# Putting a slot's four products of scores and maxima next to one another in an attention and GEGLU kernel

## The chip, the cores and the metric

The kernel runs on one core of a Trainium2 chip. Its time is device time in microseconds (us), from runs on the chip; the profile is one more execution, taken with the hardware profiler.

## The reference

For 2048 tokens of width 576 it computes a residual step with attention gated by a feed-forward network:

```
xn = layernorm(x)
s  = softmax(q k^T / sqrt(18)) v, over 32 heads of width 18, then @ wo      (q, k, v = xn @ wqkv)
g  = silu((gelu(xn @ w_gate) * (xn @ w_up)) @ w_down)                        (inner width F = 4608)
out = x + s * g
```

Everything is in float32.

## The kernel before

Float32 products are made of pieces: an operand is split into a high and a low part in TensorE's faster format, and two or three products of parts are added up. So a product with q and k takes its parts stacked in 54 rows of one tile, and one of gate or up takes three products over 64 rows for each 64 rows of the width.

**Order of the work.** A first part normalises x, makes q, k and v and stores them in DRAM. What follows is one long sequence of 144 *sections*, each of which computes one tile of 128 columns of F for one block of 512 tokens (4 blocks, 36 tiles each). The function `section` (L455) takes `gate_up` (L377) for 27 *steps*: one step is a product for `pg` on rows 0 to 63 and one for `pu` on rows 64 to 127, which run side by side. Attention is woven into these sections. TensorE's order is the order of the program (`manual_schedule` for that engine); the other engines and the DMA queues are ordered by a planner, which keeps the program's order only where `keep_in_program_order` asks for it.

**Attention.** A *unit* is four heads for one block of 512 queries; there are 32 units (NU), each with 32 *slots* (NS), eight to a section, so a unit takes four sections (NA). The softmax subtracts the true maximum of each row, so a unit's maxima are computed ahead of its scores: `LEAD` is 40 slots, five sections. The nine opening sections compute the first maxima alone (`lead_pair`), and the last five sections with attention have no maxima left. A slot has:

- two scores (`score_mm`, L716): a product `pe` of keys by queries with the negated maximum as two more rows, on rows 0 to 55 or 64 to 119, that ScalarE empties with an exp into `pT` (L725);
- two maxima (`max_mm`, L685): a product `pm` of queries by keys on rows 0 to 53 or 64 to 117, that VectorE empties with a reduce to a column of `mx` (L694).

`slot_pairs` (L732) makes two *pairs* of them: the score of one half of the rows with the maximum of the other half. Each pair is one step of TensorE. `spread` (L56) puts a section's list of specials between its 27 steps of gate and up.

**Behind the steps of a section** come, in this order on TensorE: `values` (L750), which multiplies the section's exps with v into an accumulator `acc`; in the third section of a unit `max_end` (L704), which transposes the maxima of a coming unit through a product with an identity into a `pm` (L707) that VectorE copies to `mr` (L709); at some places a part of the output projection (`project_o`); and in every second section the products with w_down (`down`, L414) of the last two tiles of F, whose `py` VectorE adds to `Y` (L431). At the last pair of F tiles of a block these are divided over two sections (`finish`, L489). `acc` goes to `accs` after four key tiles by ScalarE (L763) and afterwards by VectorE's add (L765). The activation of gate and up takes three operations each of ScalarE and VectorE (`activate`, L397; its last on VectorE is L408).

**PSUM.** There are eight buffers of 512 columns in three groups (`BANKS`): two for `pg` and `pu` (tag f), three for `pe` and `py` (tag s), three for `pm`, `acc` and `po` (tag m). A group's buffers are used in turn; a product into one waits until what its former contents were read by is done. The wait stands at the load of the product's weights.

**GpSimd** splits the weights of the next section in three tiles (`split_gu`, L93 and L95; five buffers each) and each section's activation. DMAs are issued from SyncE behind the section's steps (`load_k`, `load_v`, `load_q`) and ahead of them (`load_gu`).

Of the kernel before, what the change touches and what calls it, by code (L numbers as in the profile page):

```python
# [30 lines left out]
NU = NQ * NB  # L31
NS = 2 * NT
SLOTS = 8
# [18 lines left out]
def f(ap):  # L52
    return ap.bitcast(F32)


def spread(pairs, specials):  # L56

    n, m = len(pairs), len(specials)
    out = []
    for i in range(n):  # L60
        out += specials[i * m // n:(i + 1) * m // n]
        out.append(pairs[i])
    return out

# [2 lines left out]
def kernel(ctx: ExitStack, tc: tile.TileContext, x, wqkv, wo, w_gate, w_up, w_down, out):  # L67
    nc = tc.nc
    x = x.rearrange("b s d -> (b s) d")
    out = out.rearrange("b s d -> (b s) d")  # L70
# [35 lines left out]
    def raw_tile(shape, pool=wts):  # L106
        return pool.tile(shape, F32, name="raw", tag="raw", bufs=2)

    def load_gu(t, keep=lambda i: i):

        raw = raw_tile([P, NC, P])
        for a, w in enumerate((w_gate, w_up)):
            keep(nc.sync.dma_start(raw[HR * a:HR * a + HR], w[:, t * P:(t + 1) * P].rearrange("(k p) n -> p k n", p=HR)))
        return raw, [], []

    def split_gu(w, k):
        hi, lo = (wts.tile([P, XG, P], F32R, name=m, bufs=5) for m in ("wh", "wl"))
        split(hi, lo, w[0][:, XG * k:XG * k + XG, :])
        w[1].append(hi)
        w[2].append(lo)  # L120

    def load_xd(b):

        xd = [[], []]
        for c in range(0, NC, XG):
            for i in range(2):
                t = wts.tile([P, XG, TB], F32R, name=f"xd{i}_{c}")
                nc.sync.dma_start(f(t)[0:HR], xhs[b][i, c * HR:(c + XG) * HR, :].rearrange("(k p) t -> p k t", p=HR))
                nc.gpsimd.tensor_copy(t[HR:P], t[0:HR])
                xd[i].append(t)  # L130
        return xd
# [8 lines left out]
    with tc.tile_pool(name="pro", bufs=1) as pro, tc.tile_pool(name="pps", bufs=1, space=PSUM) as pps:  # L140
# [109 lines left out]
        def split_qk(t, raw):  # L250
            hi, lo = (pro.tile([P, KT, P], F32R, name=f"q{m}{t}") for m in "hl")
            first = split(hi, lo, raw)
            put_qk(t, hi, lo)
            return first
# [77 lines left out]
        for b in range(NB):  # L332
            for n, t in enumerate(ORDER):
                if n == (2 if b == 0 else 0) and b + 1 < NB:
                    xr = load_x(b + 1)
                if b == 0 and ahead_qk:
                    first = split_qk(*ahead_qk.pop(0))
# [39 lines left out]
    def gate_up(tag):  # L377

        w, xd = FF["w"], FF["xd"]
        pg, pu = (ps.tile([P, TB], F32, name=n, tag=tag, bufs=BANKS[tag]) for n in ("pg", "pu"))  # L380
        terms = [(wp, *divmod(c, XG), xp) for c in range(NC) for wp, xp in ((0, 0), (1, 0), (0, 1))]

        def pair(i):
            wp, k, c, xp = terms[i]
            for a, o in enumerate((pg, pu)):
                rr = slice(HR * a, HR * a + HR)
                nc.tensor.matmul(o, w[1 + wp][k][rr, c, :], xd[xp][k][rr, c, :], start=(i == 0),  # L387
                                 stop=(i == len(terms) - 1))

        return [lambda i=i: pair(i) for i in range(len(terms))], pg, pu  # L390
# [6 lines left out]
    def activate(pg, pu, early):  # L397

        t1 = ffn.tile([P, TB], F32, name="t1", bufs=2)
        nc.scalar.activation(t1, pg, AF.Square)  # L400
        nc.vector.scalar_tensor_tensor(t1, t1, 1.0 / GC, pg, op0=ALU.add, op1=ALU.mult)
        if early:
            t2 = ffn.tile([P, TB], F32, name="t2", bufs=1)
            nc.scalar.activation(t2, pu, AF.Copy)
            nc.vector.tensor_tensor(t2, t2, pg, op=ALU.mult)
        nc.scalar.activation(t1, t1, AF.Tanh, scale=GC * GS)
        if early:
            nc.vector.scalar_tensor_tensor(t1, t1, 1.0, t2, op0=ALU.add, op1=ALU.mult)  # L408
        else:
            nc.vector.scalar_tensor_tensor(t1, t1, 1.0, pg, op0=ALU.add, op1=ALU.mult)  # L410
            nc.vector.tensor_tensor(t1, t1, pu, op=ALU.mult)
        return t1
# [39 lines left out]
            nc.sync.dma_start(ys[rows, cc], th)  # L452
        FF["gates"] = []

    def section(specials=(), tag="f", raw_d=None, early=None):  # L455

        n = FF["n"]
        FF["n"] += 1
        b, r = divmod(n // G, NR)
        g = n % G  # L460
        pairs, pg, pu = gate_up(tag)
        if g == 0:
            FF["hs"] = []
        keep = tc.keep_in_program_order if n == NU * NA + len(FIRST) + 1 else lambda i: i
        nxt = load_gu((n + 1) % (NR * G), keep) if n + 1 < NF else None
        if nxt:
            for k in range(NG - 1):
                split_gu(nxt, k)
        if g == G - 1:
            raw = FF["rawd"] = raw_d() if raw_d else raw_tile([P, G, D])  # L470
            nc.sync.dma_start(raw, w_down[r * G * P:(r + 1) * G * P, :].rearrange("(g p) n -> p g n", p=P))
            if early:
                FF["wd"] = early(raw)
        for p in spread(pairs, specials):
            p()
        if nxt:
            split_gu(nxt, NG - 1)
        FF["w"] = nxt
        if n + 1 < NF and (n + 1) % (NR * G) == 0:
            FF["xd"] = load_xd(b + 1)  # L480
        FF["act"] = activate(pg, pu, n < ATT.stop)
# [118 lines left out]
    def tasks(n, part):  # L600
        for t in todo.pop((n, part), []):
            t()
# [3 lines left out]
    for b in range(NB):  # L606
# [9 lines left out]
        first = (b + 1) * AB + 3 if last else max((b + 1) * AB + 6, (b + 1) * NR * G - len(FIRST) + 5)  # L616
# [4 lines left out]
        for i in range(GROUPS):  # L621
            n = first + i * (1 if last else G)
# [17 lines left out]
    with tc.tile_pool(name="att", bufs=1, reuse_waits="tile") as att:  # L640
# [44 lines left out]
        def max_mm(u, i, a):  # L685

            if u not in MX:
                MX[u] = att.tile([P, QD, 4, 4], F32, name="mx", bufs=2)
            i, r = divmod(i, 2)
            c, t = divmod(i, 4)  # L690
            rr = slice(64 * a, 64 * a + MROW)
            pm = ps.tile([P, TB], F32, name="pm", tag="m", bufs=3)
            nc.tensor.matmul(pm, QS[u, r][rr, t * P:(t + 1) * P], KS[(u * NA + c) % KB][r][rr, :], start=True, stop=True)  # L693
            nc.vector.tensor_reduce(MX[u][:, 2 * r + a, t, c:c + 1], pm, axis=AX.X, op=ALU.max)  # L694
# [21 lines left out]
        def score_mm(u, i, a, tag="s"):  # L716

            kt, r = divmod(i, 2)
            if r == 0 and a == 0:
                PT[u, kt] = att.tile([P, QD, TB], F32, name="pT", bufs=4)  # L720
            rr = slice(64 * a, 64 * a + MROW + 2)
            pe = ps.tile([P, TB], F32, name="pe", tag=tag, bufs=BANKS[tag])
            c, t = divmod(kt, VC)
            nc.tensor.matmul(pe, KS[(u * NA + c) % KB][r][rr, t * P:(t + 1) * P], QS[u, r][rr, :], start=True, stop=True)  # L724
            nc.scalar.activation(PT[u, kt][:, 2 * r + a, :], pe, AF.Exp, scale=SCALE)  # L725
# [6 lines left out]
        def slot_pairs(s):  # L732

            u, i = divmod(s, NS)
            um, im = divmod(s + LEAD, NS)

            def pair(h):
                for a in range(2):
                    if a == h:
                        score_mm(u, i, a)  # L740
                    elif um < NU:
                        max_mm(um, im, a)

            def alone():
                for a in range(2):
                    score_mm(u, i, a, "sm"[a])

            return [lambda h=h: pair(h) for h in range(2)] if um < NU else [alone]

        def values(u, kt):  # L750
            j, g = divmod(u, NQ)
# [67 lines left out]
        for n in range(NU * NA):  # L819
            u, i = divmod(n, NA)  # L820
            s0 = n * SLOTS
            section([p for s in range(s0, s0 + SLOTS) for p in slot_pairs(s)])
            if n > 0:
                load_k(n - 1 + KB)
            if i == 1 and u + 2 < NU:
                load_q(u + 2)
            gates()
            if n == NA:
                nc.gpsimd.memset(OT, 0.0)
                nc.gpsimd.memset(f(OW[1])[HR:P, KT, :], 0.0)  # L830
            tasks(n, 0)
            um, im = divmod(s0 + LEAD + SLOTS, NS)
            if im == 0 and um <= NU:
                max_neg(um - 1)
            for kt in range(i * SLOTS // 2, (i + 1) * SLOTS // 2):
                values(u, kt)
            load_v(n + 2)
            if im == 0 and um <= NU:
                max_end(um - 1)
            tasks(n, 1)  # L840
            downs()
            tasks(n, 2)
            finish()


    with tc.tile_pool(name="epi", bufs=1, reuse_waits="tile") as epi:
# [4 lines left out]
        n = NU * NA  # L851
# [5 lines left out]
        def early(raw):  # L857
            wd = [epi.tile([P, G, D], F32R, name=m, bufs=2) for m in ("dh", "dl")]
            cut(*wd, raw)
            return wd  # L860
# [36 lines left out]
        for i in range(HIND + 1, GROUPS):  # L897
            th, j, cc = late[i]
# [31 lines left out]
```

## Time and profile before

| | us |
|---|---|
| median of three runs | 2614.52 |
| lowest and highest | 2613.62, 2616.57 |
| the profiled execution | 2613.15 |
| its span, first to last instruction | 2611.4 |

The page gives busy time by engine, the chain of work that ended last and the costliest groups of instructions. In a group, what stands before the bar is line, engine, operation, the tiles written and read, their shapes and the number of instructions; behind it are the busy time in us, the mean length of one in ns, and the idle time of the engine just before them with what ended it. A row of the timeline is start and length in us, engine, line, operation, tiles, count, and in brackets idle time before it and what ended that. PE is TensorE's products, PEld its loads of weights, DVE VectorE, ACT ScalarE, POOL GpSimd. A row of the table by windows is the window, its length, the busy time of PE, PEld, DVE, ACT and POOL with the number of their instructions, the granted clock, the DMA engines' share and GB/s. A step is written as a pair of rows (`pg` with `pu`, `pe` with `pm`) with one start time.

### The profile page before, as it was taken

How to read it: one execution, taken by the hardware profiler on the slowest of the kernel's cores; microseconds unless marked ns; L12 is line 12 of the kernel's file. 1: busy time of each engine (PE TensorE's matmuls, PEld its weight loads, DVE VectorE, ACT ScalarE, POOL GpSimd, SP SyncE). 2: the span in 40 equal slices, each digit the busy share in tenths (PEclk: the TensorE clock that was granted, in tenths of full speed). 3: DMA queues.
4: the chain of work that ended last, by engine and by line, in shares of the span. 5: the costliest groups of instructions: out<-in, count | busy, mean ns of one | idle time of the engine just before them, and what ended most of it. 6: DMA issues, size and time to landing. Idle time of an engine off the chain costs nothing.

```text
span 2611.4 us, 56340 instructions
## 1 busy us (share of the span) xinstructions
PE 2606.0 (100%) x20982; PEld 1930.9 (74%) x20982; DVE 2030.6 (78%) x3501; ACT 1506.9 (58%) x2715; POOL 1388.3 (53%) x1506
## 2 busy tenths in 40 slices
PE   9999999999999999999999999999999999999999
PEld 8888777777777777777777777777777777777778
DVE  5327888888887888888888888888888788888445
ACT  3223466666666666555666665556666765565642
POOL 2227554545466455555447655555455755555553
PEclk9999999999999999999999999999999999999999
DMA  8875434433355344544446444445345543545342
GB/s 269 261 240 155 112 102 106 103 98 103 101 126 138 101 107 107 126 112 127 104 111 149 122 106 108 120 106 138 98 108 122 140 110 100 135 110 132 81 115 58
DMA packets 392191, 324.27 MB, mean 124 GB/s; under 512 B 106540, under 2 KB 307244, under 8 KB 391920
## 3 DMA queue, kind: packets, MB, share of 16 engines
q1 hardware_dynamic: 391920, 320.68, 46.4%
q8 instruction: 168, 2.75, 0.5%
q14 instruction: 103, 0.84, 0.1%
HBM read 267.17 MB, written 52.85 MB: 123 GB/s over the span
## 4 chain that ended last, share of the span: by engine, by line
PE 99%; DMA 0%; DVE 0%; POOL 0%; SPq 0%; issue 0%; ACT 0%; POOLq 0%
PE pg L387 34%; PE py L425 18%; PE acc L759 17%; PE pm L693 9%; PE pe L724 9%; PE po L161 7%; PE po L581 2%; PE pu L387 1%; PE pt L222 0%; PE pm L707 0%; DMA raw<-in_B_w_up_dram 0%; DMA pT<-in_B_w_down_dram 0%; DMA xx<-in_A_x_dram 0%; DVE bs L190 0%; SPq L661 0%; POOL wl L95 0%
## 5 line engine op out<-in xcount | busy, mean ns | idle before, releaser
L725 ACT ACTIVATE pT<-pe 128x512 f32<-128x512 f32 x2048 | 1156.1, 599 | 704.7 <-PE pm L693 579.3
L694 DVE TENSOR_REDUCE mx<-pm 128x1 f32<-128x512 f32 x2048 | 1283.6, 683 | 84.1 <-PE pm L693 76.0
L387 PE MATMUL pg<-xd,wh 64*128 64x512 f32 x2592 | 947.6, 397 | 0.0
L387 PE MATMUL pu<-xd,wh 64*128 64x512 f32 x2592 | 947.1, 397 | 0.0
L693 PE MATMUL pm<-KS,q 54*128 54x512 f32 x2048 | 795.5, 393 | 0.0
L724 PE MATMUL pe<-q,KS 56*128 56x512 f32 x2048 | 788.1, 392 | 0.0
L387 PEld LDWEIGHTS pg<-xd,wh 64*128 64x128 f32 x2592 | 483.2, 187 | 144.5 <-issue 28.4
L93 POOL TENSOR_SCALAR wh<-raw 128x384 fp32r<-128x384 f32 x432 | 228.1, 529 | 609.7 <-PE pu L387 366.1
L387 PE MATMUL pg<-xd,wl 64*128 64x512 f32 x1296 | 508.1, 392 | 0.1
L387 PE MATMUL pu<-xd,wl 64*128 64x512 f32 x1296 | 507.7, 392 | 0.0
L387 PEld LDWEIGHTS pu<-xd,wh 64*128 64x128 f32 x2592 | 483.9, 187 | 1.7
L759 PE MATMUL acc<-pT,VS 128*32 128x512 f32 x4096 | 466.0, 595 | 0.0
L95 POOL TENSOR_TENSOR wl<-raw,wh 128x384 fp32r<-128x384 f32 x432 | 441.4, 1023 | 34.2
L693 PEld LDWEIGHTS pm<-KS,q 54*128 54x128 f32 x2048 | 377.6, 185 | 49.7 <-DVE mx L694 4.0
L724 PEld LDWEIGHTS pe<-q,KS 56*128 56x128 f32 x2048 | 372.0, 185 | 38.8
L431 DVE TENSOR_TENSOR Y<-py,Y 128x288 f32<-128x288 f32 x544 | 247.9, 457 | 161.4 <-PE py L425 161.1
L425 PE MATMUL py<-dh,hh 128*128 128x288 f32 x1152 | 346.2, 301 | 0.0
L425 PE MATMUL py<-dh,hl 128*128 128x288 f32 x1152 | 339.7, 295 | 0.0
L425 PE MATMUL py<-dl,hh 128*128 128x288 f32 x1152 | 339.5, 295 | 0.0
L759 PEld LDWEIGHTS acc<-pT,VS 128*32 128x32 f32 x4096 | 120.0, 109 | 275.7 <-issue 272.8
L387 PEld LDWEIGHTS pg<-xd,wl 64*128 64x128 f32 x1296 | 242.2, 187 | 53.6 <-POOL wl L95 0.4
L425 PEld LDWEIGHTS py<-dh,hh 128*128 128x128 f32 x1152 | 216.4, 188 | 39.4 <-issue 37.7
(127 smaller groups left out, 2966.1 us busy)
## 6 DMA issues: line engine op xcount, KB each, us to landing
KS<-qk SPq DMA_DIRECT2D x1536, 36.0 KB
raw<-in_B_w_gate_dram SPq DMA_DIRECT2D x144, 288.0 KB
raw<-in_B_w_up_dram SPq DMA_DIRECT2D x144, 288.0 KB
raw<-in_B_w_down_dram SPq DMA_DIRECT2D x68, 576.0 KB
VS<-vs SPq DMA_DIRECT2D x128, 152.0 KB
qk<-t SPq DMA_DIRECT2D x72, 256.0 KB
q<-qk SPq DMA_DIRECT2D x384, 36.0 KB
xd<-xhs SPq DMA_DIRECT2D x24, 384.0 KB
```

Source lines behind the costliest of these rows:

```text
L93: first = nc.gpsimd.tensor_scalar(hi, raw, 1.0, 1.0, op0=ALU.mult, op1=ALU.mult)
L95: keep(nc.gpsimd.tensor_tensor(lo, raw, f(hi), op=ALU.subtract))
L161: nc.tensor.matmul(o, st, m, start=(i == 0), stop=(i == len(terms) - 1))
L387: nc.tensor.matmul(o, w[1 + wp][k][rr, c, :], xd[xp][k][rr, c, :], start=(i == 0), stop=(i == len(terms) - 1))
L425: nc.tensor.matmul(py, a[:, tt], w[:, g, cc], start=(n == 0), stop=(n == 3 * G - 1))
L431: nc.vector.tensor_tensor(yy, py, yy, op=ALU.add)
L581: nc.tensor.matmul(po[:, 0:288], o[x][:, k, :], ow[w][:, k, :], start=(m == 0), stop=(m == len(terms) - 1))
L693: nc.tensor.matmul(pm, QS[u, r][rr, t * P:(t + 1) * P], KS[(u * NA + c) % KB][r][rr, :], start=True, stop=True)
L694: nc.vector.tensor_reduce(MX[u][:, 2 * r + a, t, c:c + 1], pm, axis=AX.X, op=ALU.max)
L724: nc.tensor.matmul(pe, KS[(u * NA + c) % KB][r][rr, t * P:(t + 1) * P], QS[u, r][rr, :], start=True, stop=True)
L725: nc.scalar.activation(PT[u, kt][:, 2 * r + a, :], pe, AF.Exp, scale=SCALE)
L759: nc.tensor.matmul(ACC[u][32 * a:32 * a + 32, :], VS[(u * NA + c) % VB][:, v:v + 32], pt[:, a, :], start=first, stop=last, skip_group_chec ...
```

## The change

`slot_pairs` returns one function for a slot instead of two for its pairs. `spread` takes a fixed place for the first special, and puts special i of m ahead of step `i * n // m + first`; the sections of attention call it with `first` = 1, the others as before. In the sections with maxima a slot's two pairs (score and maximum, maximum and score) thus stand next to one another, ahead of steps 1, 4, 7, 11, 14, 17, 21 and 24 of gate and up. In the five sections without maxima, where a slot is one pair of two scores, it stands at the same eight places. No product is added or removed.

```diff
-def spread(pairs, specials):
+def spread(pairs, specials, first=None):
     n, m = len(pairs), len(specials)
+    at = [-(-(i + 1) * n // m) - 1 if first is None else i * n // m + first for i in range(m)]
     out = []
     for i in range(n):
-        out += specials[i * m // n:(i + 1) * m // n]
+        out += [p for p, j in zip(specials, at) if i == j]
         out.append(pairs[i])
     return out
...
-    def section(specials=(), tag="f", raw_d=None, early=None):
+    def section(specials=(), tag="f", raw_d=None, early=None, slots=False):
...
-        for p in spread(pairs, specials):
+        for p in spread(pairs, specials, 1 if slots else None):
             p()
...
-            return [lambda h=h: pair(h) for h in range(2)] if um < NU else [alone]
+            def both():
+                for h in range(2):
+                    pair(h)
+
+            return both if um < NU else alone
...
-            section([p for s in range(s0, s0 + SLOTS) for p in slot_pairs(s)])
+            section([slot_pairs(s) for s in range(s0, s0 + SLOTS)], slots=True)
```

## The prediction

> **What bounds the kernel now.** I read the page's sums first, then the two costliest groups on the engines that empty PSUM, then the busy time of single sections, then the timeline where two sections meet.
>
> ```profile
> span 2611.4 us, 56340 instructions
> ...
> PE 2606.0 (100%) x20982; PEld 1930.9 (74%) x20982; DVE 2030.6 (78%) x3501; ACT 1506.9 (58%) x2715; POOL 1388.3 (53%) x1506
> ...
> PE 99%; DMA 0%; DVE 0%; POOL 0%; SPq 0%; issue 0%; ACT 0%; POOLq 0%
> ...
> L725 ACT ACTIVATE pT<-pe 128x512 f32<-128x512 f32 x2048 | 1156.1, 599 | 704.7 <-PE pm L693 579.3
> L694 DVE TENSOR_REDUCE mx<-pm 128x1 f32<-128x512 f32 x2048 | 1283.6, 683 | 84.1 <-PE pm L693 76.0
> ```
> ```profile
> 1302.11:1316.08 13.97, 13.97 (x120) 9.12 (x119) 13.32 (x23) 10.68 (x19) 8.35 (x8) 1.00 0.53 109
> 1316.08:1336.45 20.37, 20.37 (x168) 15.43 (x167) 16.76 (x30) 10.68 (x19) 9.77 (x11) 1.00 0.28 77
> ```
>
> TensorE is busy all the time and is 99% of the chain that ended last. A section without products of w_down (the first of the two) is 13.97 us, one with them 20.37 us, both wholly TensorE at clock 1.00. The change adds and removes no product, so it cannot shorten a TensorE that never waits; it can only leave the time alone or make TensorE wait. VectorE is the neighbour to watch: 13.32 us of work in the 13.97. So the question is whether each product still finds its PSUM buffer free.
>
> ```profile
> 1316.19 0.19 PEld L693 LDWEIGHTS pm<-KS,q 54*128 54x128 f32 x1
> 1316.42 0.19 PEld L387 LDWEIGHTS pg<-xd,wl 64*128 64x128 f32 x1
> 1316.42 0.19 PEld L387 LDWEIGHTS pu<-xd,wl 64*128 64x128 f32 x1
> 1316.65 0.19 PEld L387 LDWEIGHTS pg<-xd,wh 64*128 64x128 f32 x1
> 1316.66 0.19 PEld L387 LDWEIGHTS pu<-xd,wh 64*128 64x128 f32 x1
> 1316.89 0.18 PEld L693 LDWEIGHTS pm<-KS,q 54*128 54x128 f32 x1
> ```
> ```profile
> 1316.42 0.39 PE L693 MATMUL pm<-KS,q 54*128 54x512 f32 x1
> ```
>
> A step (two products on the two halves of the rows) follows the next after 0.2325 us (0.23 or 0.24 in the rows), whether it is of gate and up or of scores and maxima. The weights of a step are loaded one step ahead: those of the first maximum at 1316.19, its product at 1316.42. It is this load that waits for the buffer.
>
> **The change part by part.** *Order.* Before, the 16 pairs of a section stand ahead of gate/up steps 1, 3, 5, 6, 8, 10, 11, 13, 15, 16, 18, 20, 21, 23, 25, 26; after, slots of two pairs stand ahead of steps 1, 4, 7, 11, 14, 17, 21, 24. Counting both kinds, the maxima fall on steps 1, 2, 6, 7, 11, 12, 17, 18, 22, 23, 27, 28, 33, 34, 38, 39 of 43, where they fell on 1, 4, 7, 9 and so on up to 41. Steps of scores directly behind steps of scores (8 in each of 123 sections with maxima, 984) do not occur before. The nearest rows are the mixed neighbours above, 0.23 and 0.24 for 0.2325, so from 5 us less to 7 us more over all; I take nothing, since the rate did not depend on the neighbour.
>
> *Inside the slots.* Maxima have three buffers. A reduce starts 0.46 us after its product, or behind the reduce ahead of it.
>
> ```profile
> 1302.45 0.39 PE L693 MATMUL pm<-KS,q 54*128 54x512 f32 x1
> ```
> ```profile
> 1302.91 10.15 DVE L694 TENSOR_REDUCE mx<-pm 128x1 f32<-128x512 f32 x16 [0.24 <-PE pm L693]
> ```
> ```profile
> 212.87 4.28 DVE L694 TENSOR_REDUCE mx<-pm 128x1 f32<-128x512 f32 x7 [1.37 <-PE pm L693]
> ```
>
> The last row is a jammed stretch: (4.28 - 0.68) / 6 = 0.60 us from reduce to reduce. From the first maximum of a section at 0, products come at 0, 0.23, 1.16, 1.395, 2.325, 2.56. Reduces start at 0.46, 1.06, 1.66 (behind the second; its product alone would allow 1.62). A reduce frees its buffer after 0.68 + 0.06 (the 0.06 is shown below). The fourth maximum needs the first reduce, free at 1.20, which is 0.195 ahead of its product; the sixth needs the third, free at 2.40, 0.16 ahead. A longer gap of four steps then lets VectorE catch up and the pattern starts again. Five loads in a section (maxima 4, 6, 10, 12, 16) thus come 0.04 to 0.07 us later than the usual 0.2325 ahead. What does a late load cost?
>
> ```profile
> 890.14 0.68 DVE L765 TENSOR_TENSOR accs<-acc,accs 128x512 f32<-128x512 f32 x1
> ```
> ```profile
> 890.88 0.18 PEld L693 LDWEIGHTS pm<-KS,q 54*128 54x128 f32 x1 [0.16 <-DVE accs L765]
> ```
> ```profile
> 890.76 0.39 PE L387 MATMUL pu<-xd,wh 64*128 64x512 f32 x1
> 890.99 0.40 PE L693 MATMUL pm<-KS,q 54*128 54x512 f32 x1
> 891.00 0.40 PE L724 MATMUL pe<-q,KS 56*128 56x512 f32 x1
> 891.23 0.39 PE L387 MATMUL pg<-xd,wh 64*128 64x512 f32 x1
> ```
> ```profile
> 1176.30 0.18 PEld L693 LDWEIGHTS pm<-KS,q 54*128 54x128 f32 x1 [0.45 <-DVE accs L765]
> ```
> ```profile
> 1175.89 0.39 PE L387 MATMUL pu<-xd,wh 64*128 64x512 f32 x1
> 1176.30 0.50 PE L693 MATMUL pm<-KS,q 54*128 54x512 f32 x1
> 1176.64 0.39 PE L387 MATMUL pg<-xd,wh 64*128 64x512 f32 x1
> ```
> ```profile
> 1102.88:1125.10 22.22, 22.22 (x183) 17.28 (x182) 17.21 (x31) 10.68 (x19) 11.71 (x14) 1.00 0.33 94
> 1175.08:1197.60 22.52, 22.50 (x183) 17.20 (x182) 17.56 (x32) 10.68 (x19) 11.73 (x15) 1.00 0.34 100
> ```
>
> At 890 the add ended at 890.82, the load went at 890.88 (so 0.06 to release), 0.12 later than its turn at 890.76, and the steps still follow at 0.23: 0.12 is free. At 1176 the load was 0.41 late, the next step came at 1176.64 for 1176.355, and the section took 22.52 for 22.22: 0.41 - 0.12 = 0.29. So the five loads in the slots cost nothing (0.07 under 0.12), with 0.05 us to spare. ScalarE has more: an exp takes 0.60 and three buffers serve it too.
>
> The Trainium skill, TensorEngine Tiling (Array Packing), section PSUM Bottleneck, warns that packing by rows speeds TensorE but not the emptying of PSUM, so that the emptying may become the bound. That speaks against slots of four; by it the time would be that of the first rival below, by the rows the slots cost nothing.
>
> *Where two sections meet.* This is where I find the cost. In the fourth section of a unit the products of maxima come straight behind the values (no products of w_down between). The three buffers then hold the maximum of before (free), the accumulator, and the transposed maxima of the coming unit. The first maximum takes the free one; the second needs the accumulator's.
>
> ```profile
> 1316.12 0.69 DVE L765 TENSOR_TENSOR accs<-acc,accs 128x512 f32<-128x512 f32 x1
> 1316.73 0.27 DVE L709 COPY mr<-pm 32x128 f32<-32x128 f32 x1
> 1316.92 0.23 DVE L790 RECIPROCAL sums<-sums 128x16 f32<-128x16 f32 x1
> 1317.09 0.62 DVE L694 TENSOR_REDUCE mx<-pm 128x1 f32<-128x512 f32 x1
> ```
>
> The add that frees it ends at 1316.81, so the load can go at 1316.87. Today its turn is 1316.89: it fits by 0.02. After the change the second maximum is the step right behind the first, and its load's turn is 1316.42: 0.45 late, 0.12 of it free, 0.33 us lost. Everything on TensorE stands behind that load, the second score of the slot first. VectorE, 0.2 late there (its first reduce at 1317.09 for 1316.88), catches up in the pause.
>
> How often: 32 units have such a section; the last two have no maxima left to compute, and in three (one for each of the first three token blocks, at the last pair of F tiles) w_down's products stand between. That leaves 27. In two of them, the one at 1176 among them, the add is late already: VectorE's chain ahead of it ends late.
>
> ```profile
> 1175.57 0.68 DVE L765 TENSOR_TENSOR accs<-acc,accs 128x512 f32<-128x512 f32 x1
> ```
>
> The last maximum is two steps (0.47) earlier after the change, but the reduces queue; I let the chain gain 0.2 of it. Then the add starts at 1175.37, the load goes at 1176.11 for 1175.42, 0.69 - 0.12 = 0.57 lost, of which 0.29 is lost today: 0.28 each (0.48 with no gain, 0.01 with all of it). Sum: 25 x 0.33 + 2 x 0.28 = 8.8 us.
>
> *The rest.* The first third of the gate and up weights is used up one step later, and GpSimd's split that waits for that is 8.35 us of work in 13.97: covered, and 0.23 us late were it not. DMAs are issued behind the section as before. In the five sections with two products to a slot, slots come two steps earlier at the same rate, and two groups of three buffers take them: nothing. The opening sections keep their places.
>
> **The rivals.** *Evacuation becomes the bound.* If the 0.12 did not hold in slots, the five loads would cost 0.04 + 0.03 + 0.04 + 0.03 + 0.04 = 0.18 us (a stall relieves the next one), x 123 = 22 us, and the meeting 27 x 0.12 = 3 more: 2648. If reduces ran at (10.15 - 0.68) / 15 = 0.63 instead of 0.60, the sixth and twelfth loads would be 0.13 late, 0.01 to 0.02 past the cover: about 4 us, 2627. For it: only 0.05 to spare. Against: the 890 rows.
>
> *Not slower: the copy goes first.*
>
> ```profile
> 1315.90 0.25 PE L707 MATMUL pm<-identr,m 128*32 128x128 f32 x1
> ```
>
> If VectorE's order put the copy of the transposed maxima ahead of the add, it could start 0.06 after that product, at 1316.21, and with its 0.27 and 0.06 to release the buffer would be free by 1316.54, 0.12 behind the load's turn, covered; the accumulator, free at 1317.23, is then due at 1317.35. Cost nothing: 2614.5. It decides from the moment the copy starts ahead of the add. For it: their inputs are ready within 0.2 us of each other. Against: today the add goes first, and the change touches neither.
>
> *Faster: score steps behind score steps are shorter.* The break-even is 8.8 / 984 = 9 ns a step, where the rows show none under 0.23; at 0.22 it would be 984 x 0.0125 = 12 us less, 2611. The Trainium skill, TensorE: Matmul & The Clock Gate, section Back-to-back issue gap, gives 512 / 2.4 + 2.5 = 216 ns for such a product, by which it would be an estimated 2607; every step here is 0.2325, so the trace disagrees.
>
> **How the numbers follow.** The profiled execution took 2613.15 us (span 2611.4), 1.37 under the median of 2614.52. 2613.15 + 8.8 = 2621.95, and at the median 2623.3. Chances: forecast 0.73 (2619 to 2627), evacuation 0.11 (2627 to 2648), copy first 0.09, shorter steps 0.07. The forecast and the evacuation case up to 2636 hold 0.8: range 2618 to 2636. A measurement tells apart about 0.2%, 5.2 us: slower 0.84, same 0.09, faster 0.07.
>
> **What would show it.** Right: loads of maxima waiting for the add of L765 in 27 places, some 0.45 us each; sections like that of 20.37 us growing to 20.70, those of 13.97 unchanged; hundreds of short waits of such loads for L694 that cost no time. Wrong: sections of 13.97 us growing (the slots cost), L709 ahead of L765 (the copy first), or neighbouring score steps off 0.2325.

## The result and the profile after

The changed kernel takes 2622.43 us (median of 7 runs, 2621.50 to 2628.54) where the kernel before takes 2614.00 (median of 7): 1.0034 times as long, 95% interval 1.0022 to 1.0045. The forecast was 2623.3, or 1.0034 at its own median.

The page of the changed kernel (its lines stand one to five further down: L694 is the product of the maxima, L695 their reduce, L770 the add of the accumulator):

```profile
span 2626.8 us, 56338 instructions
...
PE 2615.0 (100%) x20982; PEld 1946.9 (74%) x20982; DVE 2012.3 (77%) x3501; ACT 1463.8 (56%) x2715; POOL 1387.9 (53%) x1506
...
L726 ACT ACTIVATE pT<-pe 128x512 f32<-128x512 f32 x2048 | 1111.4, 597 | 741.5 <-PE pm L694 647.6
L695 DVE TENSOR_REDUCE mx<-pm 128x1 f32<-128x512 f32 x2048 | 1260.2, 682 | 99.6 <-PE pm L694 80.6
```

This execution, 2628.54 us, is the longest of the seven by 5 us, from single long stretches that the experiments below look at again. The same number of products, and the same length of one exp and one reduce: only order and waiting differ. Two sections, the third and the fourth of the unit that was shown of before:

```profile
1311.39:1325.35 13.96, 13.96 (x120) 9.02 (x120) 12.96 (x23) 10.30 (x19) 8.60 (x9) 1.00 0.51 112
1325.35:1346.01 20.66, 20.61 (x168) 15.28 (x167) 16.70 (x30) 10.35 (x19) 9.52 (x11) 1.00 0.27 76
```

13.96 for 13.97 us, and 20.66 for 20.37. The table of waits (engine and line that waited, on whom, us in total, times, longest) names where:

```profile
PEld pm L694 <- DVE accs L770: 14.2, 27, 0.9
...
PEld pm L694 <- DVE mx L695: 3.9, 15, 0.4
```

27 loads of maxima wait for the add of the accumulator, where there were four; waits of such loads for the reduces (15 times, 16 before) are all in the opening sections. The place itself, on VectorE, the loads of weights and TensorE:

```profile
1325.39 0.69 DVE L770 TENSOR_TENSOR accs<-acc,accs 128x512 f32<-128x512 f32 x1 [0.38 <-PE acc L764]
1325.99 0.27 DVE L710 COPY mr<-pm 32x128 f32<-32x128 f32 x1
1326.19 0.23 DVE L795 RECIPROCAL sums<-sums 128x16 f32<-128x16 f32 x1
1326.35 0.62 DVE L695 TENSOR_REDUCE mx<-pm 128x1 f32<-128x512 f32 x1
```
```profile
1325.46 0.19 PEld L694 LDWEIGHTS pm<-KS,q 54*128 54x128 f32 x1
1326.13 0.18 PEld L694 LDWEIGHTS pm<-KS,q 54*128 54x128 f32 x1 [0.48 <-DVE accs L770]
```
```profile
1325.69 0.40 PE L694 MATMUL pm<-KS,q 54*128 54x512 f32 x1
1325.69 0.40 PE L725 MATMUL pe<-q,KS 56*128 56x512 f32 x1
1326.13 0.50 PE L694 MATMUL pm<-KS,q 54*128 54x512 f32 x1
1326.13 0.50 PE L725 MATMUL pe<-q,KS 56*128 56x512 f32 x1
1326.47 0.39 PE L388 MATMUL pg<-xd,wl 64*128 64x512 f32 x1
```

The second maximum's load has its turn when the first one's product starts, 1325.69. The add ends at 1326.08, the load goes at 1326.13, 0.44 late, and the step behind it starts at 1326.47 where 1325.69 + 2 x 0.2325 = 1326.155 was its time: 0.32 us lost. (This section as a whole grew by 0.29; the median of the 27 is 0.32.)

The add itself had to wait: VectorE stood idle for 0.38 us until the accumulator's last product was done. It starts 0.04 us behind the section's start, as it did before (1316.12 and 1316.08); so it is in 22 of the 27 places of either trace. There the load is late by TensorE's own order, and by these rows a faster VectorE ahead of the add would not help.

### The profile page after: what moved, and what is told of

Same layout as the page of the kernel before. It is cut to its first block, busy times and chain, and to the rows that moved or that the text cites. A ratio compares the mean times of both kernels' runs of the same rounds, so it can differ in the third digit from the quotient of the medians.

```text
span 2626.8 us, 56338 instructions
## 1 busy us (share of the span) xinstructions
PE 2615.0 (100%) x20982; PEld 1946.9 (74%) x20982; DVE 2012.3 (77%) x3501; ACT 1463.8 (56%) x2715; POOL 1387.9 (53%) x1506
## 4 chain that ended last, share of the span: by engine, by line
PE 94%; DMA 2%; POOL 1%; DVE 1%; SPq 1%; issue 0%; ACT 0%; POOLq 0%; DVEq 0%
PE pg L388 24%; PE py L426 18%; PE acc L764 16%; PE pu L388 9%; PE pm L694 9%; PE pe L725 8%; PE po L162 7%; PE po L582 2%; DMA raw<-in_B_w_up_dram 1%; DVE accs L770 1%; POOL dl L96 0%; SPq L662 0%; DMA raw<-in_B_w_gate_dram 0%; POOL wl L96 0%; PE pt L223 0%
## 5 line engine op out<-in xcount | busy, mean ns | idle before, releaser
L726 ACT ACTIVATE pT<-pe 128x512 f32<-128x512 f32 x2048 | 1111.4, 597 | 741.5 <-PE pm L694 647.6
L695 DVE TENSOR_REDUCE mx<-pm 128x1 f32<-128x512 f32 x2048 | 1260.2, 682 | 99.6 <-PE pm L694 80.6
L388 PE MATMUL pg<-xd,wh 64*128 64x512 f32 x2592 | 890.1, 398 | 0.9 <-POOL wh L94 0.9
L388 PE MATMUL pu<-xd,wh 64*128 64x512 f32 x2592 | 889.7, 398 | 0.0
L694 PE MATMUL pm<-KS,q 54*128 54x512 f32 x2048 | 643.7, 395 | 2.4 <-DVE accs L770 1.3
L725 PE MATMUL pe<-q,KS 56*128 56x512 f32 x2048 | 641.2, 393 | 0.0
L694 PEld LDWEIGHTS pm<-KS,q 54*128 54x128 f32 x2048 | 376.1, 185 | 93.3 <-DVE accs L770 14.2
L388 PEld LDWEIGHTS pu<-xd,wl 64*128 64x128 f32 x1296 | 241.4, 186 | 10.1
```

## The experiments

Theory A is the prediction's: the loss is the second maximum's load waiting for the accumulator's buffer in 27 fourth sections. Rival B: slots as such make TensorE wait for reduces, a little in each of 123 sections. Rival C: VectorE is late in the fourth section (add, copy and reciprocals stand ahead of its first reduce), whatever buffer is used.

**The first slot's pairs two steps apart, in fourth sections only.**

```diff
-            section([slot_pairs(s) for s in range(s0, s0 + SLOTS)], slots=True)
+            if i == NA - 1 and u + 2 < NU:
+                section(slot_pairs(s0, True) + [slot_pairs(s) for s in range(s0 + 1, s0 + SLOTS)],
+                        slots=[1, 3, 4, 7, 11, 14, 17, 21, 24])
```

> The changed kernel, but in the fourth section of a unit the first slot's two pairs stand ahead of steps 1 and 3, with two steps of gate and up between them; all other slots stay whole. Theory A (the second maximum's weight load waits for the accumulator's buffer): its load has its turn two steps (0.465 us) later than in the changed kernel and finds the buffer free, so the 27 sections fall from 20.69 back to 20.37 us and the time is 2614, give or take 1. Rival B (the slots as such make TensorE wait for reduces, a little in each of the 123 sections): nearly all slots are as before, so the time stays at 2622.

Measured: 2616.83 us, 1.0010 (1.0001 to 1.0020) of the kernel before in the same batch (2614.14). The section of the unit shown:

```profile
1318.33:1338.72 20.39, 20.39 (x168) 15.44 (x167) 16.57 (x30) 10.31 (x19) 9.34 (x11) 1.00 0.25 69
```

One slot of 32 taken apart gives back 5.7 of the 8.4 us, against B. But it stays 2.7 us above the kernel before, outside what was expected (2614, give or take 1). The 27 sections are 0.06 us longer than before in the median, and the attention sections have 56 waits of a maximum's load for a reduce, where the changed kernel has none; see the next run.

**The accumulator in the scores' group of buffers.** Slots stay whole everywhere.

```diff
-                ACC[u] = ps.tile([P, TB], F32, name="acc", tag="m", bufs=3)
+                ACC[u] = ps.tile([P, TB], F32, name="acc", tag="s", bufs=3)
```

> The changed kernel with the accumulator in the PSUM group of the scores (tag s) instead of that of the maxima; order of all engines as in the changed kernel. Theory A: the second maximum no longer needs the accumulator's buffer, so 2614, give or take 1, with all slots whole. Rival B (slots as such): 2622. Rival C (VectorE is late in the fourth section: add, copy and reciprocals stand ahead of its first reduce): its order is the same, so the wait moves to a later maximum of that section and the time stays at about 2622.

Measured: 2615.94, 1.0005 (0.9996 to 1.0015); the same kernel once more, as the base of a later run:

> The run with the accumulator in the scores' group once more, on the same chip as the run with early reciprocals, as its base: 2614.5 to 2616.5, fourth sections at 20.40 us.

It took 2616.14, 1.0007 (0.9998 to 1.0017) of 2614.44. So 6.6 of the 8.4 us go without touching the order: B and the strong form of C fall. The time is 0.9 us above the upper end of what was expected; neither of these two runs can be told apart from the kernel before. What is left is small and partly C's. The section, and the loads of its maxima:

```profile
1317.54:1337.94 20.40, 20.40 (x167) 15.24 (x166) 16.57 (x30) 10.31 (x19) 9.58 (x11) 1.00 0.25 76
```
```profile
1317.65 0.42 PEld L694 LDWEIGHTS pm<-KS,q 54*128 54x128 f32 x2
1318.82 0.18 PEld L694 LDWEIGHTS pm<-KS,q 54*128 54x128 f32 x1
1319.18 0.18 PEld L694 LDWEIGHTS pm<-KS,q 54*128 54x128 f32 x1 [0.18 <-DVE mx L695]
```

The first two loads go without a wait. The fourth, at 1319.18, waits for the first reduce, which the copy and the reciprocals hold back, and the section is 20.40 for 20.37.

**The first slot one step earlier, in fourth sections.**

```diff
-            section([slot_pairs(s) for s in range(s0, s0 + SLOTS)], slots=True)
+            section([slot_pairs(s) for s in range(s0, s0 + SLOTS)],
+                    slots=[0, 4, 7, 11, 14, 17, 21, 24] if i == NA - 1 and u + 2 < NU else True)
```

> The changed kernel, but in the fourth section of a unit the first slot stands ahead of step 0 instead of step 1. Theory A: the load's turn is one step earlier against an add that does not move, so each of the 27 places loses 0.55 instead of 0.32 us: sections of 20.92 us where they were 20.69, time 2628.5, give or take 1.5. Rival B (slots as such): one slot a step earlier with a longer gap behind it, 2622 or a little less.

Measured: 2629.79, 1.0059 (1.0044 to 1.0074). The slot now stands ahead of the section's first step:

```profile
1324.08 0.50 PE L725 MATMUL pe<-q,KS 56*128 56x512 f32 x1
...
1324.86 0.50 PE L694 MATMUL pm<-KS,q 54*128 54x512 f32 x1 [0.28 <-DVE accs L770]
...
1325.20 0.40 PE L388 MATMUL pg<-xd,wh 64*128 64x512 f32 x1
```

In the kernel before, a section's first step is followed by the next after 0.34 (1316.08 to 1316.42 in its trace) and that one after 0.23. So 0.57 would be due from the slot's first pair to the step behind the slot; it took 1.12: 0.55 lost, as A has it.

**One thing of the change in the kernel before.** Only the first two pairs of the fourth sections are joined.

```diff
-        for p in spread(pairs, specials):
+        order = spread(pairs, specials)
+        if join:
+            order.insert(2, order.pop(order.index(specials[1])))
+        for p in order:
             p()
```

> The kernel before with one thing of the change: in the fourth section of a unit the first two pairs stand next to each other ahead of step 1; all other pairs stay spread. Theory A: the whole cost comes with it, 27 x 0.32 = 8.6 us, so 2622.6, give or take 1, with sections of 20.69 us. Rival B (slots as such): next to nothing, 2614.

Measured: 2623.35, 1.0034 (1.0021 to 1.0046), 9.2 us more: the whole cost with 30 of the 984 new neighbours.

```profile
1321.31:1342.00 20.69, 20.64 (x167) 15.34 (x167) 16.80 (x31) 10.61 (x19) 9.89 (x11) 1.00 0.26 75
```

**The first slot's pairs one step apart.** The edit is that of the first run with places 1 and 2.

> The changed kernel, but in the fourth section of a unit the first slot's two pairs stand ahead of steps 1 and 2, with one step of gate and up between them. Theory A with its free 0.12 us: the load is 0.44 - 0.23 = 0.21 us late, of which 0.12 is free, so 0.09 us is lost in each of the 27 sections instead of 0.32; with the 0.04 us that the sections with the two pairs further apart still lost to late reduces, sections of 20.37 us become 20.46 to 20.51, and the time is 2617 to 2619. If none of the lateness were free: 0.21 lost, sections of 20.58 to 20.62, 2620 to 2622. Rival B (slots as such): 2622, like the changed kernel.

Measured: 2617.22, 1.0008 (0.9998 to 1.0018) of 2614.47.

```profile
1318.17 0.18 PEld L694 LDWEIGHTS pm<-KS,q 54*128 54x128 f32 x1 [0.25 <-DVE accs L772]
```
```profile
1317.96 0.39 PE L388 MATMUL pu<-xd,wl 64*128 64x512 f32 x1
...
1318.19 0.48 PE L694 MATMUL pm<-KS,q 54*128 54x512 f32 x1
1318.51 0.39 PE L388 MATMUL pg<-xd,wh 64*128 64x512 f32 x1
```

The load is 1318.17 - 1317.96 = 0.21 late. The step behind it comes at 1318.51 for 1317.96 + 0.465 = 1318.425: 0.085 lost, so 0.125 was free. Three places for the load, 0.44, 0.21 and less than nothing late, and the loss goes 0.32, 0.09, 0.

**The changed kernel once more.**

> The changed kernel once more, unedited, for a second profile: its first profiled execution was 5 us longer than its other runs. Theory A: 2622 to 2623, with 27 sections 0.32 us longer than before and none of the single long sections in the opening part and late in the kernel; if the 5 us belong to the change, they show again in the same sections.

Measured: 2622.84, 1.0032 (1.0021 to 1.0043). Its profile is the cleaner one:

```profile
span 2621.1 us, 56338 instructions
```
```profile
1320.05:1340.72 20.67, 20.62 (x167) 15.30 (x167) 16.70 (x30) 10.36 (x19) 9.60 (x11) 1.00 0.25 72
```

All fourth sections with maxima together are 8.7 us longer than before, for 8.8 forecast. The opening sections' 3.4 us of the first profile are gone. One long section remains: 21.34 where others like it have 20.37 (21.98 in the first profile). It waits for GpSimd's split of the activation. It is 20.66 even in the next run, whose order on TensorE is that of before, and 20.37 in the kernel before and in the run with one joint; so it is no part of what the change does to a meeting of sections. In the other runs on the changed kernel's order it is 0.24 to 1.16 us longer than before, but for the last run below (0.01). What makes it vary was not tried.

The 8.7 us are not made up as forecast. 21 of the 27 sections grew by 0.30 to 0.32 us, one by 0.38, three (at 892, 1816 and 2163 us) by 0.55 to 0.65, and the two in which the add was late before by 0.03 and 0.00.

**The kernel before with the accumulator in the scores' group.**

> The kernel before with the accumulator in the PSUM group of the scores. Theory A: in the kernel before the second maximum's load found the accumulator's buffer free by 0.02 us in all but two sections, which lost 0.29 us each; these two fall from 22.52 to 22.22 us and nothing else changes: 0.6 us less, within what a measurement can tell from no change (2613.5 for 2614.1).

Measured: 2614.49, 1.0000 (0.9990 to 1.0009). The section at 1176, of 22.52 us before:

```profile
1176.79:1199.01 22.22, 22.22 (x183) 17.28 (x182) 17.23 (x31) 10.68 (x19) 11.67 (x14) 1.00 0.34 97
```

Its 0.30 us are gone, as are those of the other late one: the same wait, in the kernel before.

**VectorE's reciprocals one section earlier,** on top of the accumulator in the scores' group.

```diff
-                    at((u + 1) * NA + 2, 2, reciprocals, u, rt)
+                    at((u + 1) * NA + 1, 2, reciprocals, u, rt)
```

> As the run with the accumulator in the scores' group, but VectorE's reciprocals of the sums are taken one section earlier (end of the second section of a unit instead of the third), so that they no longer stand ahead of the fourth section's first reduce. Theory A with what is left of rival C: the 0.03 us that those 27 sections still were over 20.37 come from VectorE starting its reduces 0.2 us late (copy and reciprocals behind the add); with the reciprocals gone the first reduce starts 0.16 earlier and 20.40 becomes 20.37 to 20.38, 0.7 us in all (2615.2 for 2615.9, at the edge of what can be told apart; the sections of the trace decide). If the 0.03 come from the slots, the sections stay at 20.40.

Measured: 2622.45, 1.0031 (1.0020 to 1.0042): a miss as a time, 6 us over its base. As a test of the 0.03 it did what A and C say together, and the rest is elsewhere:

```profile
1318.08:1338.45 20.37, 20.37 (x167) 15.70 (x167) 16.51 (x29) 10.32 (x19) 11.92 (x15) 1.00 0.34 102
2020.57:2044.80 24.23, 22.60 (x167) 16.46 (x166) 16.67 (x28) 12.35 (x23) 19.43 (x19) 0.93 0.61 145
```
```profile
2030.42 0.28 PEld L388 LDWEIGHTS pu<-xd,wh 64*128 64x128 f32 x1 [1.94 <-POOL xd L130]
```

The usual fourth section is back at 20.37, and the waits of a maximum's load for a reduce in the attention sections fall from 52 to 9, so most of the 0.03 was the late first reduce and not the slots. The second row is one of three places, two of them where a token block ends, that with the sections ahead of two of them make up the loss (7.5 us over the trace of before). There the planner, given another due time, put the work of other engines in another order. In the one quoted SyncE issues loads for the output projection (`den`, at 2006.13, 4.25 us on its queue) ahead of those of the next block's x, where the run without the edit issues them behind; GpSimd's copies of x come later, and TensorE waits for them. In the sections ahead of the other two the product that transposes the maxima waits for VectorE (L703).

## Why the prediction was right, point by point

- **What bounds.** TensorE stayed at 100% of the span; nothing but waiting could move the time. Right.
- **Inside the slots.** The sixth maximum's load was forecast 0.16 ahead of its product instead of 0.23. A slot's second pair, loads first, then products:

```profile
1314.13 0.18 PEld L694 LDWEIGHTS pm<-KS,q 54*128 54x128 f32 x1
```
```profile
1314.28 0.40 PE L725 MATMUL pe<-q,KS 56*128 56x512 f32 x1
1314.51 0.40 PE L388 MATMUL pg<-xd,wl 64*128 64x512 f32 x1
```

  The load is 0.15 ahead, and the next step follows at 0.23: late, and free. Over the 96 sections with scores and maxima that have no such meeting, the loads of maxima 4, 6, 10, 12 and 16 stand 0.19, 0.15, 0.19, 0.15 and 0.19 ahead of their products (medians) and all others 0.23: the five that were named, at the distances that were worked out. What was wrong is how it would show: hundreds of short waits of these loads for the reduces were forecast, and in the attention sections the table of waits has none, because the idle time it leaves is too short to be listed (here 0.13 us, from 1314.00, where the load before it ends, to 1314.13). It is read from the distance of load and product. A wait for a reduce does appear 123 times at another load, the accumulator's first; its idle time of 0.35 us was there before too (0.36), and it costs nothing.
- **Where two sections meet.** 0.45 late and 0.33 lost were forecast; 0.44 and 0.32 came in most of the 27 places, and the runs show that undoing either side (the order there, or the shared buffer) gives it back, and that the one joint alone brings it. The three places left out were counted rightly, but the pair of F tiles whose products stand between is the last but one of a block, not the last: in the trace of before the sections at 718.6 and 735.8 have 24 of these products each, the one at 753.0 all 48 of the next pair.
- **The two late sections.** 0.28 more each was forecast, with VectorE's chain assumed to gain 0.2 us. In the first profile it gained 0.17, and they grew from 22.51 and 22.52 to 22.81 and 22.80. In the second it gained 0.44 and they did not grow (22.54 and 22.52), nor in the run with one joint (0.01 and 0.02). Other places were late instead. One of them is in the prediction's own rows: the section at 890, whose load was 0.12 late already, was put into the sum at 0.33 and lost 0.73 in the first profile and 0.60 in the second. Which meetings have a late add differs from trace to trace, so that the sum of the second profile, 8.7 for 8.8, fits so closely is partly luck; the 0.32 of the usual places is not.
- **"VectorE catches up in the pause."** True in the changed kernel, where the 0.44 us of waiting are the pause that VectorE needs. Without that wait the fourth and sixth loads stand only 0.09 and 0.08 ahead of their products (medians of the 27), beyond the 0.12 that is free, and a section loses about 0.04 us; with the reciprocals earlier they stand 0.20 and 0.17 ahead and it loses 0.02. That is the part of rival C that holds.
- **The rivals.** Evacuation did not become the bound. The copy did not go ahead of the add (L710 stands behind L770). Scores behind scores step at 0.23 like all else (median 0.232 over 969 such steps), so the shorter step did not come.
- **Left open.** The runs with the accumulator moved or the slot apart stay 1.7 to 2.7 us above the kernel before, of which the fourth sections hold 0.8 to 1.6 in their traces and the one long section near 2050 us 0.2 to 1.2; the rest is spread in hundredths over many sections and the opening part, and was not settled.

## What to carry to other kernels

Before putting products of one kind next to each other, write down for each meeting of stages which buffer the second and third of them inherit, and from whom: in this kernel the first buffers of a shared group after a change of stage were the late ones, and the even spread was what gave them time to come free. A late load of weights cost only what went beyond 0.12 us here, about half a step, so judge a wait by the next step's start and not by the idle time shown. A sum that comes out right can hide terms that do not: compare it section by section. If the order is wanted, give the late tile another group rather than another place; here that brought it level, not ahead.

## What the runs showed of the hardware

- In the run with early reciprocals TensorE's products stood still for 1.50 us (2028.92 to 2030.42) while loads waited 0.56 and 1.94 us. Behind that the granted clock was 0.50 from 2030.5 to 2032 and 0.57 from 2032 to 2034, with loads 0.42 us apart (2031.02 and 2031.44), then 1.00 again. The section took 24.23 us where it had taken 20.37: more than the waits alone. The first profile of the changed kernel shows the same behind two stalls of 0.95 and 0.93 us at 221.6 and 223.05: a clock of 0.50 from 225 to 228. Behind single stalls of 0.70 to 0.84 us in four traces it stayed at 1.00. So a short stall can cost more than its length; where the line lies between these was not tried.
- A load of a maximum's weights that was 0.12 us late cost nothing, one that was 0.21 late cost 0.085, and one that was 0.44 late cost 0.32.
- Two executions of the changed kernel differed by 0.64 us in one single section (21.98 and 21.34) and by 3.4 us in the opening sections, which the change does not touch; a single profile can thus be 5 us off where the change is worth 8.
